# The written order of 3357 operations replaced by another in a convolution stem, forward and backward, on one core

## The chip, the cores and the metric

The kernel runs on one core of a Trainium2 chip. The metric is the device time of one launch in microseconds. Three runs of the kernel before took 1113.04, 1113.48 and 1116.73 us, median 1113.48. Five engines take part, each with its own queue of instructions that it works off in order: TensorE (PE, matmuls; its weight loads are listed as PEld), VectorE (DVE), ScalarE (ACT), GpSimd (POOL) and SyncE (SP), which here issues most of the DMAs.

## The reference

`x` is [2, 16000, 256], `w` is [31, 256, 256], `grad_out` is [2, 7985, 256], all bf16. A convolution with 31 taps and stride 2 is followed by a normalisation of each channel over the sequence and a tanh GELU; the outputs are its value and the gradients for x, w, gamma and beta.

```python
    L = (T - K) // s + 1
    h = jnp.einsum('blc,cd->bld', x[:, 0:s * L:s, :], w[0])
    for i in range(1, K):
        h = h + jnp.einsum('blc,cd->bld', x[:, i:i + s * L:s, :], w[i])
    mu = jnp.einsum('bld->bd', h)[:, None, :] / L
    var = jnp.einsum('bld->bd', (h - mu) ** 2)[:, None, :] / L
    h = (h - mu) / jnp.sqrt(var + 1e-5)
    h = h * gn_gamma[None, None, :] + gn_beta[None, None, :]
    return _gelu(h)
...
    _out, _vjp = jax.vjp(_f, x, w, gn_gamma, gn_beta)
    _grads = _vjp(grad_out)
    return (_out0, *[jnp.asarray(_g) for _g in _grads])
```

## The kernel before

The three convolutions (forward, gradient for x, gradient for w) are each cut by a fast FIR scheme: the 31 taps and the sequence are split into parts A and C and their sum B, twice nested, so that three products of half size stand for four. Products therefore need sums and differences of their operands first (VectorE) and of their results afterwards (VectorE, ScalarE).

The stages follow one another. F0 and F1 are the forward convolution of batch 0 and 1; the GELU and its derivative of batch 0 (`gelu_batch`) are worked off beside F1. Then follow G0 and G1, the gradient for x (`input_grad`), with the rest of the GELU of batch 1 beside it (`gelu_short`). W is last, the gradient for w (`weight_grad`), in nine combinations of parts; beside it, the late part of the output of batch 1 (`out0_late`) is made.

The code does not issue anything while it walks through these stages. `Plan.add` writes down each operation with its engine and a function that issues it, and finds out from the cells of SBUF and PSUM that it reads and writes which earlier operations it must follow. Then `Plan.order` reads a table, `SEQUENCE`, a list of the 3357 numbers, checks that each operation comes after those it must follow, and `emit` issues the operations in this order, held by `keep_in_program_order`. So the table alone sets the order of each engine's queue, the DMA issues on SyncE and GpSimd among them. Semaphores between engines are put in by the framework from the same dependences.

Names that the text below uses, with the lines that the profile gives:

- `load` (L314) issues a DMA, `turn` (L319) a transposing one; `x_first` (L408, L410) copies the first blocks of x, transposed by matmuls, out of PSUM.
- `w_sub` (L448) makes differences of weight parts, `f_sums` (L464) sums of x parts.
- `f_mm` (L506) issues the matmuls of the forward stage for one product: `f_leaf` the leaf products, `f_shared` those whose result two parts use. `f_copy` (L551) copies a result within PSUM on ScalarE, so that a second product can go on from it; `f_seed` (L581) does that with a VectorE pass. `f_evac` (L605, L611, L626) brings results out, with sums and squares for the statistics; `fwd_stats` (L804 to L816, root at L811) works these out.
- `keep` (L585) is ScalarE's copy of 1024 columns out of PSUM, wherever it is used.
- `w2_outer` (L1234, L1235) prepares weights for the gradient stage.
- `g_mm` (L1136) issues the matmuls of the gradient for x, `g_sums` (L1082) makes its operands. `g_copy` (L1165) is there what `f_copy` is in the forward stage: a matmul product, the copy on ScalarE, and then products that add to the copy. `g_seed` (L1199) is its VectorE form, `g_evac` (L1213, L1217) brings results out, and `load` stores them.
- `out0_late` (L964) applies GELU to a tile of batch 1 that was parked in DRAM (`hd`): load, activation on ScalarE, transposing DMA, store.
- `w_mm` (L1351) issues the matmuls of the gradient for w; `w_pairs` copies PSUM on ScalarE (L1453), `w_both` (L1461) seeds on VectorE; `leaf_d` (L1520, L1525), `pair_x` (L1417, L1421), `pair_d` (L1432, L1437) and `w_add` (L1316) make operands, and `w_emit` (L1380) brings results out. `arena` is the one SBUF buffer in which all tiles lie, `dld` and `vl` are DRAM buffers.

The loop that sets the order is

```python
        for i in self.order():
            r = self.ops[i]["fn"]()
            if hasattr(r, "__next__"):
                for ins in r:
                    pin(ins)
```

Of the kernel before, what the change touches and what calls it, by code (L numbers as in the profile page):

```python
# [39 lines left out]
7 10 4 1 11 8 5 9 2 13 3 6 12 20 14 15 36 30 38 39 29 35 32 40 33 31 24 34 37 23 41 42 50 48 47 45 21 51 44 49 46 43 22 53 59 54 26 52 64 28 60 83 84  # L40
25 65 82 18 86 85 27 66 16 62 19 67 91 17 70 55 87 79 88 58 63 92 76 251 94 56 61 57 68 89 69 180 77 95 179 71 90 177 96 73 97 98 72 242 99 178 107
100 101 194 193 102 267 108 189 93 103 127 263 116 109 190 111 141 110 78 112 104 117 113 142 114 115 143 121 198 122 105 144 74 118 119 157 124 145
123 195 75 158 126 181 153 125 183 167 197 154 146 155 159 166 156 81 160 169 162 120 163 185 147 128 182 184 164 106 80 196 165 168 176 148 175 149
150 223 161 152 222 151 187 171 204 191 170 225 129 363 199 224 203 234 213 206 130 192 273 200 361 205 271 201 255 362 214 207 132 188 209 274 377
216 133 215 131 226 366 260 275 202 210 373 211 367 212 208 287 186 218 360 227 217 219 276 220 172 134 221 324 283 277 288 325 284 285 286 233 378
293 364 292 290 228 289 295 135 279 278 232 294 231 379 280 302 281 136 296 291 282 297 326 298 137 340 299 365 138 327 301 300 380 330 328 350 139
331 368 349 374 140 336 329 381 370 333 337 338 341 339 173 351 303 264 345 376 505 332 346 344 334 372 352 343 270 353 382 507 347 174 358 348 342
383 257 229 359 369 250 230 304 386 384 387 0 305 335 385 405 306 354 506 406 417 388 307 504 407 390 389 396 392 308 418 309 371 397 355 393 258 394
520 521 400 408 375 399 402 395 431 409 310 419 247 391 415 410 411 401 420 356 404 508 414 403 398 427 416 311 422 428 357 423 312 468 429 432 313
412 421 430 425 434 510 433 441 469 511 413 235 440 314 315 443 484 316 424 523 470 442 426 436 512 444 435 437 317 471 239 516 524 438 472 439 485  # L50
446 445 475 517 474 318 509 494 319 480 473 320 321 525 476 481 486 477 478 493 482 487 483 490 479 322 489 488 323 492 522 514 491 518 496 638 503
526 495 447 532 502 497 637 531 498 530 550 519 499 636 551 552 527 533 562 528 635 553 448 529 534 500 449 537 535 563 450 536 515 576 451 564 538
539 648 541 540 554 513 546 555 639 545 547 556 542 452 640 549 453 544 559 565 548 641 543 572 566 561 577 573 454 245 593 652 568 579 642 501 567
560 643 570 574 592 578 569 575 557 594 582 656 586 558 644 581 455 571 602 585 456 583 580 584 645 587 597 237 588 457 654 591 595 589 590 598 596
611 599 621 459 607 458 460 655 600 608 601 603 612 615 605 609 610 650 620 613 646 614 616 461 606 657 617 623 622 625 618 604 633 624 619 634 462
681 682 626 683 463 663 629 658 464 662 651 653 918 665 704 659 627 672 684 628 660 664 691 668 666 466 630 631 661 467 920 649 669 676 647 670 686
465 671 678 667 924 685 677 921 687 922 680 632 679 934 690 923 688 705 673 919 730 693 941 931 674 675 930 942 689 933 692 967 932 694 926 695 696
697 698 948 935 699 925 236 940 936 700 701 702 968 703 927 707 937 708 938 709 928 943 950 929 710 969 706 711 944 714 712 957 949 966 945 713 715
946 716 947 939 954 717 953 731 726 956 733 718 955 952 719 958 965 722 720 723 725 724 721 729 973 959 734 1001 732 951 735 974 728 736 244 727 970
737 243 755 739 238 975 982 960 738 740 750 971 1007 976 252 741 991 751 972 961 986 756 742 743 978 999 992 979 744 980 758 962 745 746 754 747 981  # L60
748 988 1017 987 757 749 990 993 1024 989 759 753 241 1003 1002 780 977 752 983 1025 1004 1005 1006 760 1050 1013 985 761 984 1014 994 1000 1015 762
1016 995 1009 764 763 1008 998 765 1018 1023 776 1010 766 963 1011 767 1052 1019 783 768 1020 1012 1021 769 781 1027 772 771 770 1032 1026 773 775
774 782 779 784 1041 1028 785 1029 1022 786 1030 789 805 787 777 778 1037 1051 1036 788 790 1039 1031 1038 1034 791 1033 808 792 806 1049 1048 793
964 1042 794 799 796 795 1040 798 801 1057 1056 807 797 809 1043 830 810 1075 800 996 1053 997 811 804 1084 812 1054 1035 1065 1058 813 802 814 803
815 1055 831 816 1061 1059 817 1066 1062 1082 826 1044 1063 1077 818 1086 825 1064 1067 833 819 1071 1045 823 820 1070 824 1068 1073 821 1072 1069
832 1074 822 834 1083 857 827 1060 835 828 829 836 1101 1076 1091 1087 1085 1088 1089 1092 837 1090 1097 839 1096 838 1078 1099 840 1093 1046 1098
841 850 1094 1047 842 1103 268 1106 1081 1102 843 851 1095 1115 844 860 1100 846 854 1107 859 1116 1108 848 845 849 1136 861 1135 855 1114 1110 1118
847 858 862 1104 853 856 1111 863 1112 1125 884 866 864 852 1109 1134 1113 865 867 1120 1119 1079 868 1133 1122 1105 869 1121 1127 1124 1123 1117
1132 1131 870 885 871 1146 876 883 1126 877 873 874 875 1128 878 1145 886 1144 872 888 256 1141 887 889 1142 1170 1080 890 881 879 1148 1162 880 1143
1172 882 891 893 892 1153 1149 894 1154 895 1150 904 1151 1147 896 1163 905 1155 1156 897 1152 1157 898 1158 1165 1173 899 1159 1164 1137 1160 900  # L70
1161 1166 1174 1274 1171 906 907 901 1169 1175 1196 253 902 1195 1176 1198 1186 1182 1138 1197 903 1183 1184 1178 1185 1275 1202 1129 1289 1177 1203
1199 1180 1179 908 1291 909 1204 1292 1187 1276 1139 1191 910 1277 1189 1181 1192 1190 1205 1130 911 1200 1188 1193 1206 912 1140 1297 1167 1194 1298
1215 913 1201 1281 914 1219 1229 1216 1217 1208 1218 915 1278 1231 916 1294 1228 1293 1220 1207 1295 1230 1221 1168 1210 1296 1300 1321 1224 1299
1320 1212 1225 1290 1243 1213 1303 1226 1232 1301 1337 1227 1222 269 1302 1304 1209 1282 1244 1305 1306 1211 1523 1252 1214 1251 1223 1234 1254 1233
1235 1236 1358 1246 1285 1256 1237 1245 1239 1279 1238 1240 1241 1247 1524 1253 1323 1249 1248 1308 1255 1309 1250 1311 1242 1257 1312 1284 1260 1258
1313 1283 1261 1287 1310 1525 1259 1322 1526 1262 1280 1263 1531 1264 1527 1265 1532 1266 1324 1267 1315 1533 1325 1307 1327 1314 1268 1570 1537 1269
1318 1270 1271 1272 1316 1273 1317 1538 1571 1339 1539 1551 1319 1341 1326 1336 1543 1340 1528 1342 1529 1338 1288 1534 1530 1343 1544 1573 1572 1328
1286 1344 1578 1541 1345 1545 1329 1575 1542 1540 1346 1535 1330 1574 1548 1549 1331 1536 1579 1547 1347 1334 1550 1553 1648 1348 1649 1362 1349 1582
1559 1360 1350 1587 1580 1558 1352 1332 1583 1576 1552 1581 1356 1566 1586 1577 917 1546 1355 1554 1357 1560 1361 1565 1651 1555 1353 1363 1556 1650
1359 1606 1652 1561 1557 1364 1660 1607 1333 1564 1354 1585 1366 1563 1584 1562 1379 1589 1612 1365 1569 1335 1611 1629 1608 1653 1367 1630 1609 1654  # L80
1567 1655 1614 1590 1610 1368 1613 246 1616 1617 1595 1628 1369 1625 1618 1591 1370 1383 1623 1615 1371 1568 1598 1622 1657 1620 1656 1627 1594 1373
1381 1593 1619 1599 1631 1588 1377 1592 1624 1351 1658 1375 1378 1664 1376 1636 1384 1626 1380 1643 1601 1621 1382 1600 1665 1596 1632 1374 1385 1661
1637 1597 1633 1400 1668 1386 1712 1659 1674 1634 1387 1789 1644 1602 1635 1638 1388 1603 1641 1645 1666 1711 1389 1639 1667 1642 1790 1390 1640 1720
1404 1672 1647 1604 1673 1372 1391 1646 1669 1678 1719 1713 1670 1392 1605 1402 1675 1715 1394 1671 1676 1716 1679 1685 1398 1680 1399 1397 1684 1682
1681 1686 1403 1690 1792 1401 1405 1692 1795 1662 1714 1683 1406 1677 1724 1722 1691 1794 1408 1407 1663 1721 1393 1718 1688 1693 1717 1689 1409 1793
# [1608 lines left out]
```

## Time and profile before

| what | value |
|---|---|
| runs, median (lowest to highest) | 1113.48 us (1113.04 to 1116.73) |
| profiled execution, span | 1111.2 us |
| instructions in it | 18967 |
| VectorE busy | 919.9 us, 83% |
| ScalarE busy | 578.9 us, 52% |
| GpSimd busy | 129.3 us, 12% |
| DMA packets, volume | 348806, 256.16 MB |
| share of the 16 DMA engines, SyncE's hardware queue | 81.8% |
| granted TensorE clock | 1.00 in every stretch quoted below |

Of the profiled execution the page gives the span; the times of runs contain, beside the span, what lies around it. Busy times count an engine's instructions; TensorE's own row is quoted in the prediction. In rows of groups and of the timeline, brackets or the part behind the last bar tell how long the engine stood idle just before, and what it waited for. In a row of windows, each engine has its busy time and in parentheses its instructions.

### The profile page before, as it was taken

What the parts mean: (1) busy time and instruction counts of PE and PEld (TensorE: products, weight loads), DVE (VectorE), ACT (ScalarE), POOL (GpSimd) and SP (SyncE); (2) the same over time, 40 slices, a digit from 0 to 9 for tenths busy, and PEclk for the clock granted to TensorE, in tenths of its full rate; (3) what the DMA queues carried; (4) which work ended last, traced back from release to release, by engine and by line L of the source; (5) the groups of instructions that cost most, each with busy time, mean ns of one, the idle gap of its engine ahead of it and who ended that gap; (6) DMA issues with size and microseconds to landing.
All of it is one profiled execution on the core that took longest, in us unless ns stands there. A gap on an engine that the chain in (4) does not pass through costs nothing.

```text
span 1111.2 us, 18967 instructions
## 1 busy us (share of the span) xinstructions
PE 1086.2 (98%) x7623; PEld 749.8 (67%) x7672; DVE 919.9 (83%) x900; ACT 578.9 (52%) x880; POOL 129.3 (12%) x233
## 2 busy tenths in 40 slices
PE   6999999999999989999999999999999999999998
PEld 4888899878787974444444444444587776678885
DVE  7987877889999999989897565644789699699995
ACT  1234434587988569899964566545413322111221
POOL 0000000000001003232332432251200000000000
PEclk9999999999999999999999999999999999999999
DMA  9979899876969789999999898577994959978888
GB/s 231 198 188 249 233 275 267 219 167 162 209 166 219 240 328 270 274 252 265 217 225 237 179 203 183 157 201 197 278 293 137 270 156 298 303 254 279 282 253 207
DMA packets 348806, 256.16 MB, mean 231 GB/s; under 512 B 234327, under 2 KB 315869, under 8 KB 343517
## 3 DMA queue, kind: packets, MB, share of 16 engines
q1 hardware_dynamic: 341613, 236.05, 81.8%
q0 software_dynamic: 7104, 18.89, 6.3%
q8 instruction: 60, 0.98, 0.4%
q14 instruction: 29, 0.24, 0.1%
HBM read 114.62 MB, written 84.45 MB: 179 GB/s over the span
## 4 chain that ended last, share of the span: by engine, by line
PE 89%; DVE 5%; issue 2%; DMA 1%; SPq 1%; ACT 1%; DVEq 0%
PE ps L1136 34%; PE ps L506 34%; PE ps L1351 21%; SPq L314 1%; DMA out_dram<-arena 1%; DVE arena L1437 1%; DVE ps L1461 1%; DMA arena<-in_w_dram 1%; DVE arena L1421 1%; DVE arena L1380 1%; DVE arena L1525 0%; DVE arena L581 0%; DVE arena L1417 0%; DVE arena L448 0%; DVE arena L1316 0%
## 5 line engine op out<-in xcount | busy, mean ns | idle before, releaser
L506 PE MATMUL ps<-arena 128*128 128x256 bf16 (+4 forms) x3464 | 396.6, 278 | 11.2 <-DMA arena<-in_x_dram 4.7
L1136 PE MATMUL ps<-arena 128*128 128x512 bf16 (+1 forms) x1787 | 388.1, 376 | 5.7 <-ACT ps L1165 3.6
L506 PEld LDWEIGHTS <-arena 128*128 128x128 bf16 x3464 | 338.2, 98 | 69.4 <-DMA arena<-in_x_dram 5.8
L1136 PEld LDWEIGHTS <-arena 128*128 128x128 bf16 x1824 | 178.5, 98 | 215.1 <-issue 2.9
L1351 PE MATMUL ps<-arena 128*128 128x256 bf16 (+1 forms) x2372 | 301.6, 289 | 3.4 <-DVE arena L1520 1.8
L1351 PEld LDWEIGHTS <-arena 128*128 128x128 bf16 x2384 | 233.2, 98 | 71.9 <-issue 2.3
L585 ACT ACTIVATE arena<-ps 128x1024 bf16<-128x1024 f32 (+1 forms) x121 | 122.1, 1022 | 213.0 <-PE ps L1351 77.3
L464 DVE TENSOR_TENSOR arena<-arena 128x2064 bf16<-128x2064 bf16 (+7 forms) x131 | 162.7, 1265 | 24.2 <-PE ps L506 23.0
L314 POOL DMA_DIRECT2D dld<-arena x144 | 104.6, 728 | 246.7 <-DMA arena<-arena 229.4
L1199 DVE TENSOR_TENSOR ps<-ps,arena 128x1024 f32<-128x1024 f32 x36 | 44.3, 1232 | 64.2 <-PE ps L1136 53.2
L1082 DVE TENSOR_TENSOR arena<-arena 128x1032 bf16<-128x1032 bf16 (+1 forms) x114 | 89.5, 813 | 9.5 <-POOL arena L1049 4.3
L551 ACT ACTIVATE ps<-ps 128x256 f32<-128x256 f32 x89 | 36.7, 412 | 85.6 <-PE ps L506 84.5
L1316 DVE TENSOR_TENSOR arena<-arena 128x4096 bf16<-128x4096 bf16 x30 | 68.3, 2287 | 0.5 <-DMA arena<-in_x_dram 0.3
L1165 ACT COPY ps<-ps 128x512 f32<-128x512 f32 x84 | 48.1, 575 | 33.7 <-PE ps L1136 30.0
L323 POOL MEMSET arena<- 128x104 bf16 (+11 forms) x52 | 12.0, 249 | 414.8 <-DVE arena L464 157.6
L923 DVE TENSOR_TENSOR arena<-arena 128x2048 bf16<-128x2048 bf16 (+1 forms) x48 | 57.5, 1197 | 3.0 <-ACT arena L926 1.3
L605 ACT ACTIVATE arena<-ps 128x512 bf16<-128x512 f32 (+1 forms) x64 | 37.0, 582 | 32.7 <-PE ps L506 28.2
L885 DVE TENSOR_TENSOR arena<-arena 128x2048 bf16<-128x2048 bf16 (+1 forms) x40 | 47.7, 1197 | 4.0 <-ACT arena L879 1.7
L1437 DVE TENSOR_TENSOR arena<-arena 128x2048 bf16<-128x2048 bf16 x40 | 48.5, 1220 | 2.4 <-PE ps L1351 2.4
L1461 DVE TENSOR_TENSOR ps<-ps,arena 128x1024 f32<-128x1024 f32 x24 | 29.1, 1227 | 19.5 <-PE ps L1351 19.5
L1453 ACT COPY ps<-ps 128x256 f32<-128x256 f32 x54 | 19.0, 360 | 47.8 <-PE ps L1351 46.7
L1525 DVE TENSOR_TENSOR arena<-arena 128x4608 bf16<-128x4608 bf16 x16 | 40.6, 2554 | 0.0
(92 smaller groups left out, 752.3 us busy)
## 6 DMA issues: line engine op xcount, KB each, us to landing
arena<-in_x_dram SPq DMA_DIRECT2D x36, 1024.0 KB
arena<-hd SPq DMA_DIRECT2D x40, 512.0 KB
dld<-arena POOLq DMA_DIRECT2D x144, 128.0 KB, 4.4
out_dram<-arena SPq DMA_DIRECT2D x14, 1024.0 KB
arena<-dld SPq DMA_DIRECT2D x18, 640.0 KB
arena<-dld SPq DMA_DIRECT2D x18, 576.0 KB
vl<-arena SPq DMA_DIRECT2D x36, 256.0 KB
arena<-vl SPq DMA_DIRECT2D x9, 1024.0 KB
```

What stands on the lines that cost most here:

```text
L314: lambda: e.dma_start(out=out, in_=in_), dma=np_ * ns / 16e3 * 1.03, ns=ns, tp=SH[pk], slack=slack)
L464: lambda: nc.vector.tensor_tensor(out=o, in0=a, in1=b, op=ALU.add))
L506: yield nc.tensor.matmul(ps[:, dh, cs], lhsT=wt, rhs=mv, start=s0, stop=False, skip_group_check=True)
L585: lambda: nc.scalar.activation(out=out, in_=ps, func=ACT.Copy, scale=scale))
L885: add("DVE", dve(nf), [o], [a, b_], lambda: V.tensor_tensor(out=o, in0=a, in1=b_, op=op))
L923: add("DVE", dve(nf), [o], [a, b_], lambda: V.tensor_tensor(out=o, in0=a, in1=b_, op=op))
L1082: lambda: nc.vector.tensor_tensor(out=o, in0=a, in1=b, op=ALU.subtract))
L1136: yield nc.tensor.matmul(ps[:, e, 0:wide], lhsT=lt, rhs=mv, start=s0, stop=False, skip_group_check=True)
L1165: add("ACT", act(512), [o], [i], lambda: nc.scalar.copy(out=o, in_=i))
L1316: add("DVE", dve(4096), [o], [a, b], lambda: nc.vector.tensor_tensor(out=o, in0=a, in1=b, op=ALU.add))
L1351: yield nc.tensor.matmul(ps[:, s, c0:c1], lhsT=lt, rhs=mv, start=s0, stop=False, skip_group_check=True)
L1437: add("DVE", dve(2048), [o], [u, v], lambda o=o, u=u, v=v: nc.vector.tensor_tensor(out=o, in0=u, in1=v, op=ALU.subtract))
```

## The change

All 105 lines of the table are replaced by another permutation of the same 3357 numbers. Operations, dependences, buffers and all other code are the same. The first line of the table, before and after, stands for all:

```diff
 SEQUENCE = """
-7 10 4 1 11 8 5 9 2 13 3 6 12 20 14 15 36 30 38 39 29 35 32 40 33 31 24 34 37 23 41 42 50 48 47 45 21 51 44 49 46 43 22 53 59 54 26 52 64 28 60 83 84
+12 1 2 10 5 4 8 11 20 13 6 7 3 9 14 15 30 33 29 39 32 31 35 38 36 40 37 23 34 48 47 44 45 21 49 42 51 46 41 50 43 52 53 28 59 54 24 65 22 64 60 84 26
...
```

What moves is shown at three places. A row is one instruction or several alike (x and their number), with its line, operation, output and input.

SyncE, the start of the program: loads of x, of w and the first transposing loads. Before:

```order
L314 DMA arena<-in_x_dram 128x4x512 x2
L314 DMA arena<-in_x_dram 16x4x512
L314 DMA arena<-in_w_dram 128x4x256 x4
L314 DMA arena<-in_w_dram 128x3x256
L314 DMA arena<-in_w_dram 128x4x256 x4
```

and now:

```order
L314 DMA arena<-in_w_dram 128x4x256
L314 DMA arena<-in_x_dram 128x4x512 x2
L314 DMA arena<-in_w_dram 128x4x256
L314 DMA arena<-in_x_dram 16x4x512
L314 DMA arena<-in_w_dram 128x4x256 x4
```

One load of w has moved ahead of the two large first loads of x, and another ahead of the small one.

ScalarE, from the end of the forward convolution into the gradient for x. Before:

```order
L605 ACTIVATE arena,hsum_109<-ps 128x2x230 x3
L626 ACTIVATE arena,hsq_111<-arena 128x1024
L1165 COPY ps<-ps 128x512
L626 ACTIVATE arena,hsq_111<-arena 128x1024 x2
L1165 COPY ps<-ps 128x512
L1235 ACTIVATE arena<-arena 128x2048
L811 ACT_TABLE_LOAD
L811 ACTIVATE small<-small,eps_t 128x2
L1165 COPY ps<-ps 128x512
L585 ACTIVATE ps<-ps 128x1024
L1165 COPY arena<-ps 128x512
L916 ACTIVATE arena<-arena,stats 128x1024 x4
```

and now:

```order
L605 ACTIVATE arena,hsum_109<-ps 128x2x230 x2
L1165 COPY ps<-ps 128x512 x2
L626 ACTIVATE arena,hsq_111<-arena 128x1024 x2
L1165 COPY arena<-ps 128x512
L1165 COPY ps<-ps 128x512
L811 ACT_TABLE_LOAD
L811 ACTIVATE small<-small,eps_t 128x2
L585 ACTIVATE ps<-ps 128x1024
L916 ACTIVATE arena<-arena,stats 128x1024 x4
```

The two first copies now stand together ahead of the two squares, the copy to `arena` and the third copy stand ahead of the table load, and the pass of L1235 has moved out of the piece to an earlier place. On TensorE, whose rows all read alike here, the products were, by what they feed: first copy's producer, its consumer, second copy's producer, its two consumers, the third copy's producer, its two consumers. Now they are: first producer, second producer, a product of the outer part, a consumer of the second copy, the consumer of the first (the third copy's producer), the other consumer of the second, the two consumers of the third. At 485 us, too, a product has moved between the producer and the consumer of a copy, and at 199 us the four products that feed a seed (L581) have moved ahead of five others.

ScalarE, from the gradient for x (L585, L1165) into the gradient for w (L1453). Before:

```order
L1165 COPY ps<-ps 128x512 x2
L1165 COPY arena<-ps 128x512 x2
L585 ACTIVATE arena<-ps 128x2x512 x4
L1453 COPY ps<-ps 128x256 x6
L585 ACTIVATE arena<-ps 128x1024 x4
L1453 COPY ps<-ps 128x256
L585 ACTIVATE arena<-ps 128x1024
L1453 COPY ps<-ps 128x256 x5
L585 ACTIVATE arena<-ps 128x1024
L964 ACT_TABLE_LOAD
L964 ACTIVATE arena<-arena,stats 128x1024
```

and now:

```order
L1165 COPY arena<-ps 128x512
L585 ACTIVATE arena<-ps 128x2x512 x2
L964 ACT_TABLE_LOAD
L964 ACTIVATE arena<-arena,stats 128x1024
L585 ACTIVATE arena<-ps 128x2x512 x2
L1453 COPY ps<-ps 128x256 x6
L585 ACTIVATE arena<-ps 128x1024 x3
L964 ACTIVATE arena<-arena,stats 128x1024
```

The first activation of `out0_late` and the table load that it needs have moved from behind the copies of the second combination of W to between the last two pairs of evacuations of the gradient for x. Its load from `hd` has moved with it on SyncE, ahead of a load of the d tile.

208 rows, old and new, of the table SEQUENCE are left out of this document.

## The prediction

> **What bounds the kernel now.** I read the page first (span, busy times, chain), then the waits of TensorE, then the chain and the timeline around each long wait. Columns of the busy line: busy us, share of the span, instructions.
>
> ```profile
> span 1111.2 us, 18967 instructions
> PE 1086.2 (98%) x7623; PEld 749.8 (67%) x7672; DVE 919.9 (83%) x900; ACT 578.9 (52%) x880; POOL 129.3 (12%) x233
> PE 89%; DVE 5%; issue 2%; DMA 1%; SPq 1%; ACT 1%; DVEq 0%
> ```
>
> TensorE is busy 1086.2 of 1111.2 us and carries 89% of the chain that ended last. The change leaves all operations as they are, so those 1086 us stay. Only the rest can shrink: 1111.2 − 1086.2 = 25.0 us. Its named part is in the waits of TensorE (us in total, times, longest):
>
> ```profile
> PE ps L506 <- DMA arena<-in_x_dram: 4.7, 1, 4.7
> PE ps L1136 <- ACT ps L1165: 3.6, 4, 1.1
> PE ps L1351 <- DVE arena L1520: 1.8, 1, 1.8
> PE ps L506 <- DVE arena L448: 1.7, 2, 1.1
> PE ps L506 <- DVE ps L581: 1.4, 1, 1.4
> PE ps L506 <- DVE arena L464: 1.3, 1, 1.3
> PE ps L1351 <- DVE arena L1421: 1.0, 1, 1.0
> PE ps L506 <- DVE arena L410: 0.7, 1, 0.7
> PE ps L506 <- ACT arena L408: 0.7, 1, 0.7
> PE ps L506 <- ACT ps L551: 0.7, 1, 0.7
> ```
>
> These sum to 17.6 us. Of them 4.7 is the first load, before which nothing can be multiplied. The last stretch of matmuls in the timeline (start, length, what, count, idle before) is
>
> ```profile
> 1073.30 33.20 PE L1351 MATMUL ps<-arena 128*128 128x256 bf16 x238 [0.99 <-DVE arena L1421]
> ```
>
> and ends at 1106.5, so another 4.7 us is the tail. What a better order can win is therefore the other 12.9 us at most, 1.2% of the span. No wait but the first names a DMA directly. The wait for L1520 has one behind it, below. A plan that only gives transfers more room finds little to win here; what it moves for that can cost.
>
> **The change, place by place.** Base is the profiled execution, span 1111.2; the median of the runs, 1113.48, lies 2.3 us above it, which I take as the time around the span and the same for both kernels. So each term is added to 1113.5.
>
> *Start (0 to 37 us).* In SyncE's new order one load of w stands ahead of the two first loads of x. The first issues, two waits of TensorE, and the page's row of ScalarE's copies (busy, mean ns, idle before):
>
> ```profile
> 0.74 2.04 SPq L314 DMA_DIRECT2D arena<-in_x_dram  x3
> 16.28 9.18 PE L506 MATMUL ps<-arena 128*128 128x512 bf16 x60 [1.08 <-DVE arena L448]
> 26.06 10.67 PE L506 MATMUL ps<-arena 128*128 128x256 bf16 x88 [0.60 <-DVE arena L448]
> L551 ACT ACTIVATE ps<-ps 128x256 f32<-128x256 f32 x89 | 36.7, 412 | 85.6 <-PE ps L506 84.5
> ```
>
> Three issues in 2.04 are 0.68 us each, so the first x lands about 0.7 later, and 256 KB of w share the engines with it: +0.7. On TensorE two short leaf products (8 matmuls of 256 columns, 8 × 10.67 / 88 = 1.0 us each) now stand in the wait at 16.28. They need less than what they are put ahead of, but VectorE must still make its operands; of the 1.08 I leave 0.5. A leaf product of twice that length is moved up ahead of 26.06 and covers that wait, 0.6. But the leaf product that stood behind the shared product at 26.06, as cover for ScalarE's copies of it (L551, 412 ns), is now later, so the next products follow the shared one directly and wait for two copies and the handover: +1.0, bounded by the present 0.7 for L551 and three copies, 1.2. Sum 0.7 − 0.6 − 0.6 + 1.0 = **+0.5** (−0.6 to +1.5).
>
> *Second forward batch (199 us).*
>
> ```profile
> 197.77 1.23 DVE L581 TENSOR_TENSOR ps<-arena,ps 128x1024 f32<-128x1024 f32 x1 [0.52 <-PE ps L506]
> 199.06 2.15 PE L506 MATMUL ps<-arena 128*128 128x231 bf16 x20 [1.39 <-DVE ps L581]
> ```
>
> VectorE's seed starts after the last product on that PSUM and TensorE has nothing but its consumer. The new order does that group first and puts five other products between, of 8 matmuls like those of the row (8 × 2.15 / 20 = 0.86 us), 4.3 in all: the 1.39 goes. What is late next is another product seeded by a second 1.23 us pass, behind one product; I leave 0.3 for it. **−1.1** (−1.4 to −0.6).
>
> *From forward to input gradient (407 to 418 us).* Pieces of the chain that ended last here (start, length, what):
>
> ```profile
> 409.95 1.15 ACT arena L626 x2
> ...
> 412.27 0.48 ACT ps L1165
> 412.75 1.84 ACT arena L1235
> 414.59 0.02 issue
> 414.61 1.28 ACT L811
> ```
>
> ScalarE paces it: squares for the statistics (L626), one 1.84 us pass (L1235) and a table load (L811) stand ahead of copies (L1165) that TensorE waits for. Three waits of the 3.6 us row lie here, 2.9 in all (the fourth, 0.7, is at 485). The new order puts L1235 some 14 rows earlier on ScalarE, joins the two first copies ahead of two squares, and puts other products between a copy's producer and consumer on TensorE. What is left: on ScalarE the third copy to ps stands behind the first two, two squares and a copy to arena. From the last forward product on the second copy cannot end before two products and itself, 2 × 0.86 + 0.57 = 2.3; the squares add 2.2 and the next two copies 1.2, 5.7 us in all. TensorE has six products of four matmuls, 0.86 each (working below), before it needs the third copy, 5.2: 0.5 left. Then the table load, its root and a keep of 1.02 end some 2.6 after it, with two products, 1.7, as cover: 0.9 left if all of that comes in a row, 0 if the keep is early, taken 0.5. So 1.0 of 2.9 stays: **−1.9** (−2.9 to −0.3).
>
> *At 485 us.*
>
> ```profile
> 484.89 0.57 ACT L1165 COPY ps<-ps 128x512 f32<-128x512 f32 x1 [0.40 <-PE ps L1136]
> 485.51 2.75 PE L1136 MATMUL ps<-arena 128*128 128x512 bf16 x11 [0.66 <-ACT ps L1165]
> ```
>
> The consumer of the copy stood right behind its producer; now one product stands between: **−0.7** (−0.8 to 0).
>
> *The rest of the input gradient.* This is where the new order gives something back. Windows (us, busy and instructions of PE, PEld, DVE, ACT, POOL, clock, DMA share, GB/s):
>
> ```profile
> 417.00:475.00 58.00, 57.74 (x270) 26.70 (x274) 56.53 (x66) 52.24 (x59) 17.91 (x25) 1.00 1.07 272
> 490.00:797.00 307.00, 305.53 (x1411) 140.83 (x1439) 206.41 (x236) 196.57 (x254) 92.73 (x162) 1.00 0.87 211
> ```
>
> TensorE loses 1.5 us in 307 now. A four-matmul product is 4 × 57.74 / 270 = 0.86; a copy with its handovers cost TensorE 0.66 of waiting at 485.51. Before, most consumers of a copy have two products between them and their producer, about 1.7 us; in the new order some 45 have exactly one. One product just covers a copy when ScalarE is free, and does not when a keep (L585, 1.02 us in the rows below) has just begun. ScalarE is busy 196.57 of 307 us here, 64%. None of the 45 may collide (0), or one in ten for a whole keep (4.5). The order puts copies ahead of keeps at most of these places, so I take the end nearest to the present row, one collision: **+1.0** (0 to +4.5).
>
> *From input gradient to weight gradient (797 to 816 us).*
>
> ```profile
> 802.78 1.24 DVE arena L1213
> 804.02 0.02 issue
> 804.03 6.89 DMA out_dram<-arena
> ```
>
> then two passes of L1520 and the 1.75 us wait of TensorE at 813.92. Keep, evacuation, store, buffer free, d planes: this chain has no slack (the keep at 801.73 is quoted below). In the new order ScalarE gets a table load and the first late GELU (L964) between the two pairs of keeps at its head. Present prices and present gaps:
>
> ```profile
> L964 ACT ACTIVATE arena<-arena,stats x16: 1224/1240/1263, 842.2 to 1092.8; 128x1024 bf16<-128x1024 bf16 x16
> L964 ACT ACT_TABLE_LOAD  x1: 1283/1283/1283, 840.9 to 840.9; - x1
>   DMA arena<-hd: 31.2, 2
> 800.00 1.02 ACT L585 ACTIVATE arena<-ps 128x1024 bf16<-128x1024 f32 x1 [0.65 <-PE ps L1136]
> 801.73 1.02 ACT L585 ACTIVATE arena<-ps 128x1024 bf16<-128x1024 f32 x1 [0.70 <-PE ps L1136]
> ```
>
> 1.28 + 1.24 = 2.52, less the two gaps 0.65 + 0.70 = 1.35, leaves 1.2 by which the second keep, and with it the store and TensorE's wait, is late; 0.1 more for three copies behind it. At 840 the same pair delayed nobody. **+1.3** (0, if the store no longer ends last, to +5, rival two).
>
> The Trainium skill ("ScalarE: Activation LUTs", section "What ACT_TABLE_LOAD costs") gives 1283 ns for the load and about 1380 ns for a drain with it. By that, an estimate, this term would be +2.7 and the time 1114.0. This case's trace has the 1283 ns and no drain: the first GELU began at 842.2, 1.3 us after the load at 840.9.
>
> *VectorE's stretch and the tail.*
>
> ```profile
> 1000.00:1073.00 73.00, 72.30 (x634) 61.84 (x632) 72.66 (x54) 13.64 (x21) 0.00 (x0) 1.00 0.85 274
> ```
>
> VectorE is full (72.66 of 73) and the wait of 1.0 at 1073 is its. The same passes must come before the same product, so an order can neither help nor harm: 0 (−0.9 to +1). The tail, 4.7 us, is the last evacuation and stores and stays.
>
> Sum: 0.5 − 1.1 − 1.9 − 0.7 + 1.0 + 1.3 = −0.9, so 1113.5 − 0.9 = 1112.6.
>
> **The rivals.** *One: the waits go and nothing comes back.* For it: all of the waits removed are short round trips, and the new order does put products into each. Against it: the one-product distances and L964 in the chain. Without the two plus terms, and with all 2.9 at 407 to 418 gone: 0.5 − 1.1 − 2.9 − 0.7 = −4.2, 1109.3.
>
> *Two, slower: the load behind L964.*
>
> ```profile
> 797.00:816.00 19.00, 17.20 (x137) 13.30 (x137) 15.75 (x14) 8.07 (x12) 2.88 (x4) 1.00 1.03 229
> ```
>
> ScalarE takes its queue in order. The GELU needs a 512 KB load from hd, issued shortly before 797. If it has not landed when the keep ahead of it ends (799.4), ScalarE stands, and the next keeps, the evacuation, the store and TensorE's wait are late by the same time. ScalarE waited 31.2 us in two such waits before, without harm since nothing hung on it; by this window's row the DMA engines move 229 GB/s at a share of 1.03 in this stretch, so 512 KB take 2.3 us. One such length late, and the store's 6.89 longer by another: 1.3 + 2.3 + 2.3 = 5.9 in place of 1.3, so 1112.6 + 4.6 = 1117.2; with three or four collisions in the input gradient too, 1120. It decides from a lateness of 2.1 us that the store shares: 2 × 2.1 takes 1112.6 over 1116.8. Against it: the new order puts the load on SyncE ahead of the last loads of the d tile for the next stage, so it has several us before 799.4.
>
> *Three: the order misses its plan.* Loads and stores on SyncE's queue are moved by up to hundreds of us; one that now lands late makes a wait that the trace of before cannot show. Each would cost 1 to 3 us, and collisions of copies and keeps add to them: 1114 to 1119. If the waits also stay where they are because real times differ from the plan's, the time is 1113.5.
>
> **How the numbers follow.** Chances: forecast (1110.2 to 1116) 0.40; rival one (1106 to 1110.1) 0.30; rival two (1117 to 1121) 0.15; rival three 0.15, half of it within 0.3% and half above. A measurement of this kernel tells about 0.3% from no change, 3.3 us, so faster is below 1110.1 and slower above 1116.8: faster 0.30, same 0.40 + 0.08 = 0.48, slower 0.15 + 0.07 = 0.22. The range 1107 to 1119 leaves out the best third of rival one and the upper half of rival two, less than 2 in 10.
>
> **What would show it.** The waits of TensorE: L581 no longer at 1.4; L1165 from 3.6 to below 2 around 408 to 418, but with new short entries between 490 and 797; L1520 grown from 1.8 to about 3; L551 with a second entry near 28 us; the first load later than 4.68. VectorE's and ScalarE's busy times must be unchanged. If L1520's wait is gone or not longer, the term for L964 is wrong; if ScalarE stands more than 2 us for hd near 800, rival two holds; if a DMA is named among TensorE's waits after the first, rival three. Wrong altogether would be a time below 1106, since it would need the matmul work itself or the tail to shrink.

## The result and the profile after

| | before | changed |
|---|---|---|
| runs, median (lowest to highest) | 1114.14 us (1113.04 to 1116.73) | 1132.56 us (1128.09 to 1134.99) |
| profiled execution, span | 1111.2 us | 1133.2 us |
| ratio to before, 95% interval | | 1.0157 (1.0132 to 1.0183) |

The new order is 1.6% slower, 18 us, where no change was forecast and the range ended at 1119. (The kernel before has four runs here; its median over three, 1113.48, is what the prediction starts from.) First the page of the changed kernel, then the waits of TensorE (us in total, times, longest):

```profile
span 1133.2 us, 18998 instructions
PE 1092.2 (96%) x7622; PEld 749.9 (66%) x7672; DVE 925.3 (82%) x900; ACT 581.8 (51%) x880; POOL 127.7 (11%) x233
```

```profile
PE ps L1136 <- DVE ps L1199: 7.6, 5, 5.6
PE ps L506 <- DMA arena<-in_x_dram: 6.3, 1, 6.3
PE ps L1136 <- ACT ps L1165: 2.7, 4, 1.4
PE ps L1136 <- ACT arena L585: 2.5, 2, 1.4
PE ps L506 <- DVE arena L464: 2.5, 3, 1.9
PE ps L1136 <- DVE arena L1217: 2.4, 2, 1.4
PE ps L506 <- ACT ps L551: 2.2, 3, 0.9
PE ps L1351 <- DVE arena L1520: 1.4, 1, 1.4
PE ps L1136 <- DVE stats L987: 1.0, 1, 1.0
...
PE ps L506 <- DVE ps L581: 0.8, 1, 0.8
```

What was 3.6 us for L1136 is now a whole family: the seed L1199, the copy L1165, the keep L585, the evacuation L1217, and more. Still no DMA but the first load is named. The window of the gradient for x, from its first product to the first of the gradient for w, shows where the time lies (columns as in the prediction; before, then changed):

```profile
408.02:801.52 393.50, 387.96 (x1787) 178.59 (x1825) 290.39 (x339) 274.80 (x345) 118.22 (x201) 1.00 0.91 225
```

```profile
410.39:823.99 413.60, 393.30 (x1789) 178.62 (x1824) 293.35 (x340) 275.48 (x348) 117.90 (x203) 0.99 0.88 219
```

413.6 against 393.5: 20.1 us of the 22.0 by which the spans differ. TensorE is idle for 20.3 of them in place of 5.5, and its busy time is 5.3 longer for the same products, some of which ran at a lower granted clock (last section). Ahead of this stage the new order is 2.4 late, behind it 0.5 early.

So one asks what VectorE and ScalarE waited for in this stretch. Before, their waits name no DMA at all; two rows name GpSimd (4.3 and 1.6 us). In the changed kernel, VectorE's and ScalarE's waits between 410 and 824 us:

```profile
DVE arena L1316 <- DMA arena<-in_x_dram: 9.2, 1, 9.2
DVE arena L1017 <- DMA arena<-dyd: 6.6, 4, 2.0
DVE arena L1015 <- DMA arena<-hd: 3.4, 2, 2.3
DVE arena L1217 <- DMA out_dram<-arena: 3.0, 1, 3.0
DVE arena L1082 <- DMA arena<-arena: 2.1, 1, 2.1
DVE arena L1234 <- DMA dld<-arena: 1.4, 1, 1.4
ACT arena L916 <- DMA arena<-hd: 4.6, 2, 3.8
ACT arena L1024 <- DMA arena<-dyd: 3.2, 2, 2.5
ACT L964 <- DMA arena<-hd: 2.2, 1, 2.2
```

These sum to 35.7 us. GpSimd is named for 12.9 us, where it was 5.9. Here is one of the waits for a load, in SyncE's and ScalarE's timeline of the changed kernel:

```profile
666.59 0.58 SPq L314 DMA_DIRECT2D arena<-dyd  x1
```

```profile
670.33 1.15 ACT L1024 ACTIVATE arena<-arena,stats 128x1024 bf16<-128x1024 bf16 x1 [2.51 <-DMA arena<-dyd]
671.38 1.92 ACT L585 ACTIVATE arena<-ps 128x1024 bf16<-128x1024 f32 x2
```

The load is issued at 666.59, its first user could run 1.2 us later, when ScalarE was free, and starts 3.7 later. Two keeps stand behind it on ScalarE, and TensorE waits 1.1 us for the first. Before, the same load went out 7.1 us ahead of the first operation that needs it, and ScalarE did not wait:

```profile
645.21 0.32 SPq L314 DMA_DIRECT2D arena<-dyd  x1
```

```profile
652.29 1.16 ACT L1024 ACTIVATE arena<-arena,stats 128x1024 bf16<-128x1024 bf16 x1
```

The longest wait, in the chain that ended last and on TensorE's timeline of the changed kernel:

```profile
803.35 11.47 DMA arena<-in_x_dram
...
814.91 0.06 DVE arena L1316
814.97 2.15 issue
817.12 1.23 DVE ps L1199
```

```profile
818.40 5.76 PE L1136 MATMUL ps<-arena 128*128 128x512 bf16 x16 [5.63 <-DVE ps L1199]
```

A sum for the gradient for w (L1316) waits for a load of x that takes 11.5 us beside two others of 1 MB, and the last seed of the gradient for x (L1199) stands behind it on VectorE. VectorE was free for the sum at 805.69, 2.3 us after the load went out at 803.35. Before, the same load had 9.0 us, and the sum did not wait:

```profile
787.28 0.58 SPq L314 DMA_DIRECT2D arena<-in_x_dram  x1
```

```profile
796.24 2.28 DVE L1316 TENSOR_TENSOR arena<-arena 128x4096 bf16<-128x4096 bf16 x1
```

### The profile page after: what moved, and what is told of

It reads as the page before. It is cut to its first block, busy times and chain, and to the rows that moved or that the text cites. A ratio compares the mean times of both kernels' runs of the same rounds, so it can differ in the third digit from the quotient of the medians.

```text
span 1133.2 us, 18998 instructions
## 1 busy us (share of the span) xinstructions
PE 1092.2 (96%) x7622; PEld 749.9 (66%) x7672; DVE 925.3 (82%) x900; ACT 581.8 (51%) x880; POOL 127.7 (11%) x233
## 5 line engine op out<-in xcount | busy, mean ns | idle before, releaser
L1136 PE MATMUL ps<-arena 128*128 128x512 bf16 (+1 forms) x1787 | 393.5, 378 | 20.3 <-DVE ps L1199 7.6
L1136 PEld LDWEIGHTS <-arena 128*128 128x128 bf16 x1824 | 178.6, 98 | 234.8 <-issue 25.2
L585 ACT ACTIVATE arena<-ps 128x1024 bf16<-128x1024 f32 (+1 forms) x121 | 121.3, 1021 | 221.3 <-PE ps L1351 90.9
L464 DVE TENSOR_TENSOR arena<-arena 128x2064 bf16<-128x2064 bf16 (+8 forms) x131 | 163.1, 1263 | 10.7 <-PE ps L506 6.3
L1082 DVE TENSOR_TENSOR arena<-arena 128x1032 bf16<-128x1032 bf16 (+1 forms) x114 | 89.5, 813 | 19.1 <-PE ps L1136 8.7
L1316 DVE TENSOR_TENSOR arena<-arena 128x4096 bf16<-128x4096 bf16 x30 | 68.2, 2284 | 20.4 <-DMA arena<-in_x_dram 20.1
L1199 DVE TENSOR_TENSOR ps<-ps,arena 128x1024 f32<-128x1024 f32 x36 | 44.2, 1229 | 39.2 <-PE ps L1136 27.6
L1165 ACT COPY ps<-ps 128x512 f32<-128x512 f32 x84 | 48.0, 573 | 38.7 <-PE ps L1136 35.7
L551 ACT ACTIVATE ps<-ps 128x256 f32<-128x256 f32 (+1 forms) x89 | 36.3, 410 | 59.8 <-PE ps L506 58.3
L323 POOL MEMSET arena<- 128x78 bf16 (+11 forms) x52 | 11.4, 244 | 377.7 <-DVE arena L885 151.2
L1437 DVE TENSOR_TENSOR arena<-arena 128x2048 bf16<-128x2048 bf16 x40 | 48.2, 1217 | 5.2 <-PE ps L1351 4.8
L964 ACT ACTIVATE arena<-arena,stats 128x1024 bf16<-128x1024 bf16 x16 | 19.3, 1236 | 54.2 <-DMA arena<-hd 54.2
L1213 DVE TENSOR_TENSOR arena<-arena 128x2048 bf16<-128x2048 bf16 x20 | 24.4, 1221 | 24.3 <-ACT arena L585 24.3
```

Source lines behind the costliest of these rows:

```text
L464: lambda: nc.vector.tensor_tensor(out=o, in0=a, in1=b, op=ALU.add))
L585: lambda: nc.scalar.activation(out=out, in_=ps, func=ACT.Copy, scale=scale))
L1082: lambda: nc.vector.tensor_tensor(out=o, in0=a, in1=b, op=ALU.subtract))
L1136: yield nc.tensor.matmul(ps[:, e, 0:wide], lhsT=lt, rhs=mv, start=s0, stop=False, skip_group_check=True)
L1165: add("ACT", act(512), [o], [i], lambda: nc.scalar.copy(out=o, in_=i))
L1316: add("DVE", dve(4096), [o], [a, b], lambda: nc.vector.tensor_tensor(out=o, in0=a, in1=b, op=ALU.add))
```

## The experiments

**Which stage.** Four splices of the two orders: up to a cut one order, from there the other. The first has its cut at operation 1311, the first product of the gradient for x; a piece of the table around it, old order, then spliced:

```diff
-1248 1308 1255 1309 1250 1311 1242 1257 1312 1284
+1280 1283 1527 1242 1284 1311 1287 1533 1525 1257
```

*e1*, old, then new.

> The order of before up to the first product of the gradient for x (407 us), the new order from there to the end. Theory one (the loss lies in the gradient for x: from its first to its last product the new order took 413.5 us, the old 393.3) expects about +20 us over the kernel before, within 4. Rival (the loss starts in the forward stage, where the new order was already 2.3 us late, and is carried on) expects +10 or less.

Measured: 1131.57 us against 1113.81, ratio 1.016 (1.0137 to 1.0183): +18. *e3*, the other way round at the same cut:

> The new order up to the first product of the gradient for x, the old order from there. Theory one expects +0 to +3 us against the kernel before: 2.3 late at that place, of which the old order behind it gives nothing back. Rival (the leftover of the forward stage sets the gradient's waits) expects +10 us or more.

Measured: 1114.94, ratio 1.0007 (0.9997 to 1.0018). So at most some 2 us of the 18 begin in the forward stage. *e16* goes over to the old order only at 1970, in the middle of the gradient for x:

```diff
-1915 1982 1511 1512 1988 1970 2027 1983 1939 2026
+1981 1913 1915 1982 1988 1970 2027 1983 1939 2026
```

> The new order to the end of the gradient for x of batch 0 (575 us), the old order from there. By the stages of the traces (new against old: forward +2.3, batch 0 +4.7, batch 1 +15.5, gradient for w -0.5) theory two expects +5 to +8 us. Rival (the loss of batch 1 comes from leftovers of batch 0) expects +15 us or more.

Measured: 1123.6 against 1114.09, ratio 1.0094 (1.0079 to 1.0109), +9.5, somewhat more than the 5 to 8 that were expected and far from the rival's 15. About half of the loss stands by the end of batch 0, so both batches lose. *e2* takes the old order up to the first product of the gradient for w, 2771:

```diff
-2751 2750 2752 2782 2780 2771 2753 2783 2776 2754
+2705 2707 2872 2875 2704 2771 2753 2781 2708 2776
```

> The order of before up to the first product of the gradient for w (801 us), the new order from there. Theory one (nothing lost in the gradient for w, 309.4 against 309.9 us) expects -1 to +1 us against the kernel before. Rival (the new order's loads for this stage come too late whatever stood ahead) expects +3 us or more.

Measured: 1125.71, ratio 1.011 (1.0095 to 1.0125): +12, where -1 to +1 was expected. The cut made it: the load from hd (2872) that the new order issues ahead of this stage now goes out behind the cut, with its GELU (2875) close behind. One of TensorE's waits in e2, and what ScalarE did:

```profile
PE ps L1351 <- ACT ps L1453: 10.8, 1, 10.8
```

```profile
813.06 1.28 ACT L964 ACT_TABLE_LOAD   x1 [10.46 <-DMA arena<-hd]
```

The copies of L1453 stood behind L964, which waited for its load. This is the prediction's second rival, as an artefact of the splice. It says nothing on the new order's last stage, which in the trace of the changed kernel takes 0.5 us less than before.

**Heads of queues.** The first theory was that operations which wait for a transfer merely stand ahead of what TensorE needs. *e4* swaps two operations on VectorE:

```diff
-L1199 TENSOR_TENSOR ps<-ps,arena 128x1024
-L1316 TENSOR_TENSOR arena<-arena 128x4096
-L1199 TENSOR_TENSOR ps<-ps,arena 128x1024
+L1199 TENSOR_TENSOR ps<-ps,arena 128x1024 x2
+L1316 TENSOR_TENSOR arena<-arena 128x4096
```

> The new order with one operation moved by one place on VectorE: the sum of x blocks for the gradient for w (L1316), which waited 9.2 us for its load with the last seed but one of the gradient for x (L1199) behind it, goes behind that seed. Theory one (one sum at the head of the queue costs the 5.6 us wait of TensorE at 818 and the 2.3 us by which the next 16 matmuls ran slower) expects 7 to 9 us less than the changed kernel, so about +10 us over the kernel before, and a granted clock of 1.00. Rival (the load is late anyway, and the wait moves to the first product of the gradient for w that needs the sum) expects 2 us less or nothing.

Measured: 1133.17 (1127.96 to 1139.77), nothing gained. The 5.6 us wait is gone from the trace, but the next one has grown, from 1.4 us:

```profile
PE ps L1351 <- DVE arena L1520: 4.1, 1, 4.1
```

*e5* mends six such places further up; two of the six as rows:

```diff
-L1017 TENSOR_SCALAR arena<-arena,stats 128x2048
 L1217 TENSOR_TENSOR arena<-ps,arena 128x2x512
+L1017 TENSOR_SCALAR arena<-arena,stats 128x2048
...
-L1024 ACTIVATE arena<-arena,stats 128x1024
 L585 ACTIVATE arena<-ps 128x2x512 x2
+L1024 ACTIVATE arena<-arena,stats 128x1024
```

> The new order with six places of the gradient for x mended, the boundary to the gradient for w left alone. At each, an operation that waits for a transfer steps behind the evacuation, seed or copy that stood behind it: on VectorE L1017 twice (waited 2.0 and 1.7 us for a load), L1015 to L1033 once (1.1), on ScalarE L1024 (2.5), on GpSimd two stores behind three fills (VectorE waited 1.6 for them); and on SyncE a store to out_dram goes ahead of three transposing loads (VectorE waited 3.0 for it). Theory one (each of these waits was handed on to TensorE whole or in part: 1.05, 1.03, 0.95, 1.12, 1.41 and 1.39 us there) expects 5 to 8 us less than the changed kernel, about 1126. Rival (VectorE and ScalarE are simply too full in this stretch, and another wait of the same size takes each place) expects 2 us less or nothing.

Measured: 1132.1. *e6*, e4 and the late GELU:

```diff
-L964 ACT_TABLE_LOAD
-L964 ACTIVATE arena<-arena,stats 128x1024
 L585 ACTIVATE arena<-ps 128x2x512 x2
 L1453 COPY ps<-ps 128x256 x6
+L964 ACT_TABLE_LOAD
+L964 ACTIVATE arena<-arena,stats 128x1024
```

> The new order with the sum of L1316 behind the seed, as in e4_swap_back, and the first late GELU (L964), with its table load, behind the six copies of L1453 instead of ahead of two keeps. Theory one (queue heads that wait for a load: what e4 took away at 818 us partly came back as a longer wait at 828, since the keeps stand behind L964, whose load from hd lands late in some runs) expects 1124 to 1127 us and a spread of runs below 5 us, where e4 had 1128 to 1140. Rival (the store of the last evacuation and the loads of x land late by themselves) expects the 1128 to 1140 of e4 again.

Measured: 1135.02 (1128.4 to 1135.72). *e7*, e5 and e6 together:

> The new order with the edits of e5 and e6 together. Theory one expects the sum of both, 1132 - 6 - 7, about 1118 to 1121 us; the rest over the kernel before is then the later start (1.6) and waits that were not mended (L1235 at 587, 1.4 to 2.5). Rival (too much work at these places) expects no more than the better of the two.

Measured: 1135.6 (1130.87 to 1139.88). Theory one fell three times over. In e6's trace the waits at the mended places are gone or short, and TensorE waits at the first products of the gradient for w instead, for L1520 and for loads of that stage by name:

```profile
PE ps L1351 <- DVE arena L1520: 5.8, 1, 5.8
PE ps L1351 <- DMA arena<-dld: 3.4, 2, 2.0
```

**Transfers.** Theory two: the transfers themselves are late. *e9* sorts the queues of SyncE and GpSimd between 410 and 830 us by readiness; 180 of SyncE's operations and 165 of GpSimd's move, by 10 places at most. The first piece:

```diff
-L314 DMA arena<-vl_57 128x4096
+L314 DMA arena<-hd_0_64 128x2x1024
+L314 DMA arena<-vl_57 128x4096 x2
 L314 DMA hd_3_67<-arena 128x4096
-L314 DMA arena<-hd_0_64 128x2x1024
```

> The new order with only the queues of SyncE and GpSimd sorted anew between 410 and 830 us: each load, transposing load and store goes out in the order in which its inputs or its buffer were ready in the trace of the changed kernel (at most 12 us ahead of where it stood); the queues of TensorE, VectorE and ScalarE stay. Theory two (mending heads of queues did nothing because the transfers themselves are issued too late: VectorE and ScalarE waited 0 us for DMAs in the gradient for x before, and 36 us now; leads of 6.6 to 15.7 us before are 0.9 to 5.8 now, while a load needs 5 to 8) expects 5 to 10 us less than the changed kernel, for those transfers that stood ready behind others. Rival (they are late because the new order of VectorE and ScalarE sets their buffers free too late, so no order on SyncE helps) expects within 2 us of the changed kernel.

Measured: 1133.25, ratio 1.0175 (1.0158 to 1.0193). But the lateness is still there: the waits of VectorE and ScalarE for DMAs in this stretch sum to 32 us, where the changed kernel had 36. *e10*, e9 and e7 together:

> The edits of e9 and of e7 together: transfers in order of readiness, and what waits for one behind what TensorE waits for. Theory two expects less than e9, about 1117 to 1122 us, since now both the lateness and its handing on are cut. Rival (buffers too late) expects the 1131 to 1140 us of e7.

Measured: 1133.01. Sorting SyncE's and GpSimd's queues gives nothing back either, as the rivals of e9 and e10 had it. *e12* goes the other way and makes the old order late; two of its twelve moves, both on SyncE, are *e15*. The second of these two is:

```diff
-L319 DMA_TRANSPOSE arena<-arena 128x4x128 x8
-L314 DMA arena<-dyd_2_74 128x2048
-L319 DMA_TRANSPOSE arena<-arena 128x4x128
+L319 DMA_TRANSPOSE arena<-arena 128x4x128 x9
 L314 DMA out_dram<-arena 104x4096
 L319 DMA_TRANSPOSE arena<-arena 128x4x128 x2
 L314 DMA arena<-hd_2_66 128x2048
 L314 DMA dld_7_83<-zt_114 2x256
-L319 DMA_TRANSPOSE arena<-arena 128x4x128 x5
+L319 DMA_TRANSPOSE arena<-arena 128x4x128 x4
+L314 DMA arena<-dyd_2_74 128x2048
+L319 DMA_TRANSPOSE arena<-arena 128x4x128
```

> The order of before with eleven transfers of the gradient for x on SyncE and one on GpSimd moved back in their queue by 0 to 10 places, by the time that their lead over their user is shorter in the new order (2.6 to 14.7 us); all compute queues stay. Theory two expects waits of VectorE and ScalarE for these transfers as in the changed kernel, some 10 to 20 us in all, and 4 to 10 us more than the kernel before. Rival (the new order of the compute queues is what costs) expects 0 to 1 us more.

Measured: 1129.54 against 1114.13, ratio 1.0131 (1.0099 to 1.0163): +15, more than the 4 to 10 expected. The waits of VectorE and ScalarE for DMAs sum to 17 us, as expected.

> The order of before with two of the twelve transfers of e12 moved back alone: a load of hd for the GELU (by 3 places on SyncE) and a load of dyd (by 10). In e12 TensorE waited 4.2 and 5.5 us behind these two, and ran at a granted clock of 0.75 and 0.54 for the 5.5 us after each. Theory (a wait of 4 us or more is paid about one and a half times) expects 9.7 of waits and 3 to 4 of slow clock, +11 to +14 us over the kernel before. Rival (the loss of e12 comes from all twelve together) expects +3 us or less.

Measured: 1122.78 against 1114.09, ratio 1.0087 (1.0066 to 1.0107): +8.7 for two loads out of 3357 operations, less than the 11 to 14 expected and far more than the rival's 3. The waits were shorter than in e12: in e15 TensorE waited 3.9 and 3.0 us for the keeps behind the two loads' users:

```profile
PE ps L1136 <- ACT arena L585: 3.9, 1, 3.9
PE ps L1136 <- ACT ps L585: 3.0, 1, 3.0
```

**The loads taken away.** *e13* is the new order without 42 loads, *e14* the old one without them (line numbers of both are 3 higher from `emit` on):

```diff
+        leave = set([1291, 1292, 1298, 1320,
...
         for i in self.order():
+            if i in leave:
+                continue
```

> The new order without 42 loads that VectorE and ScalarE wait for in the gradient for x: those of dyd and hd for its operands and its GELU, and the last two of x and the first of hd for the gradient for w. What they would fetch is left out, and the operations go on with what the tiles hold. Theory two (late loads are the cause) expects most of the 20 us back: within 2 to 6 us of e14. Rival (the order of the compute queues is the cause) expects 12 to 18 us more than e14.

> The order of before without the same 42 loads, as a control for e13. Both theories expect no change against the kernel before, within 1 us, since VectorE and ScalarE waited for no DMA in this stretch.

Measured, against 1114.09: e13 1116.15, ratio 1.0017 (1.0007 to 1.0027); e14 1114.53, ratio 0.9999 (0.9988 to 1.0011). The control does not move, and 16 of the 18 us are gone. GpSimd, too, is named for 3.3 us in place of 12.9. TensorE's timeline of e13, up to the gradient for w:

```profile
411.47 2.83 PE L1139 MATMUL ps<-arena 128*128 128x512 bf16 x11
...
433.52 370.87 PE L1139 MATMUL ps<-arena 128*128 128x512 bf16 x1697 [0.17 <-DVE arena L923]
804.23 10.64 PE L1354 MATMUL ps<-arena 128*128 128x256 bf16 x96
```

From 433.5 to 804.2 not one wait of TensorE is listed. The stage takes 392.8 us, where the old order takes 393.5. So the new order of VectorE, ScalarE and TensorE is as good as the old one there, the one-product distances included, once the loads are out of it. That the loads cost by coming late, and not only by their volume, is what e12 and e15 show: all their loads are there, and only places in a queue differ.

**Moves to keep?** *e8* took two of the new order's moves on TensorE, the first of them in part, into the old order (numbers of operations in TensorE's queue):

```diff
-612 620 616 617 623 622 618 619 681
+612 620 616 617 618 619 623 622 681
...
-1689 1695 1702
+1695 1689 1702
```

> The order of before with two of the new order's moves on TensorE alone: at 199 us the four products that feed the seed (L581) go ahead of two others, and at 485 us one product goes between a copy (L1165) and its producer. Theory (these two waits, 1.39 and 0.66 us, go and nothing comes back) expects 1.5 to 2 us less than the kernel before. Rival (the wait at 199 only moves, as the new order showed 0.8 us at another seed, at 219) expects 0 to 1 us less.

Measured: 1116.97 against 1113.95, ratio 1.0025 (1.0015 to 1.0035), 3 us more. The wait at 199 us grew by 1.0, since VectorE's queue kept a sum (L464) that needs operation 622 ahead of the seed, and the granted clock behind it was 0.72 for 5.5 us, 1.5 us more (last section). At 485 us a wait of 0.5 for an evacuation (L1217) took the place of the 0.66 for the copy. Both in TensorE's waits in e8:

```profile
PE ps L506 <- DVE ps L581: 2.4, 1, 2.4
...
PE ps L1136 <- DVE arena L1217: 0.5, 1, 0.5
```

*e11* moves the seed too, and leaves out the move at 485:

```diff
-L464 TENSOR_TENSOR arena<-arena 128x8x232
-L581 TENSOR_TENSOR ps<-arena,ps 128x1024
+L581 TENSOR_TENSOR ps<-arena,ps 128x1024
+L464 TENSOR_TENSOR arena<-arena 128x8x232
```

> The order of before with the move at 199 us done on both queues: the four products that feed the seed (L581) go ahead of two others on TensorE, and on VectorE the seed goes ahead of the sum (L464) that waits for one of those two. In e8 only TensorE's part was moved, and its wait there grew from 1.39 to 2.35 us behind that sum. Theory (the wait at 199 is a plain round trip) expects 1 to 1.4 us less than the kernel before. Rival expects no change.

Measured: 1113.03 against 1114.13, ratio 0.9992 (0.9983 to 1.0001). The row for L581 is gone from TensorE's waits; the row for L464 grew from 1.3 to 1.9. This is the best version found, but its interval reaches no change.

## Why the prediction was wrong

- *What bounds the kernel*: the products stay, but "those 1086 us stay" was wrong: TensorE is busy 1092.2 us in the new order, in part because of the lower granted clock behind the longest wait. Whether 12.9 us can be won no run shows; the best version (e11) has a median 1.1 lower, with an interval that reaches no change. I wrote that "No wait but the first names a DMA directly" and drew from it that transfers had room to spare. They had some, and that room was the thing at stake: a reserve does not show as a wait until it is gone.
- *Start*, +0.5: the terms were off and the sum close. The first load came 1.6 us later (6.3 against 4.7), not 0.7; both waits for L448 went, where half of one was to stay; L551 got its second wait, 0.92 at 30.22, as forecast. At the wait that both orders share, 37.41 became 38.05: +0.6.
- *199 us*, −1.1: the wait of 1.39 went. A seed elsewhere took 0.8 (L581), a miss of the kind "what is late next" in another place than I looked. All told the forward stage came out 2.4 later, not 0.6 earlier; e3 puts it at 1.1, with an interval that reaches no change.
- *407 to 418 us*, −1.9: right. Of 2.9 for L1165 there, 0.8 is left, 0.25 named for L1082 and 0.57 for the keep L585; I had said 1.0. *485 us*, −0.7: that wait went.
- *The rest of the input gradient*, +1.0, at most +4.5: **this is the step that failed.** I counted distances between copies and products and let ScalarE's keeps collide with copies. e13 shows that the one-product distances cost nothing. What I did not count is the distance between each load and its first user, in queue places on SyncE against queue places on VectorE and ScalarE; the sum has no term for it, and only rival three speaks of it. For the load of dyd above, 7.1 us became 1.2, for the load of x 9.0 became 2.3. The stage from the first product of the gradient for x to the first of the gradient for w lost 20 us, and TensorE's waits for what stood behind such loads, with the clock they cost, are what e13 took away.
- *From input gradient to weight gradient*, +1.3: the wait for L1520 shrank (1.75 to 1.38) instead of growing to 3, so by the prediction's own sign the term was wrong. A larger wait, 5.6 us, came 18 us earlier, at a seed behind L1316. L964 with its table load was not what bound there: ScalarE waited 2.2 for its load, inside TensorE's longer wait for the seed. (More than 2 us was the sign for rival two; the wait came, but it is not what TensorE waited for.) The Trainium skill ("ScalarE: Activation LUTs", section "What ACT_TABLE_LOAD costs") puts a drain of about 1380 ns beside the table load. None showed here either: the load takes 1.28 us and the GELU follows it at once, in ScalarE's timeline:

```profile
816.33 1.28 ACT L964 ACT_TABLE_LOAD   x1 [2.23 <-DMA arena<-hd]
817.62 1.24 ACT L964 ACTIVATE arena<-arena,stats 128x1024 bf16<-128x1024 bf16 x1
```

- *VectorE's stretch and the tail*, 0: right; from the first product of the gradient for w to the end the new order takes 0.5 us less, of which L1520 has 0.4. The busy times of VectorE and ScalarE, forecast as unchanged, rose by 5.4 and 2.9 us; no run looks into that.
- *The rivals*: the second had the mechanism, a load at the head of an in-order queue with TensorE's work behind it, at one place and at 1117. The third, "the order misses its plan", had the cause, with 0.15 and at most 1119: I priced a few late loads, there were a dozen, and I took a wait's price for its length. Its sign for the reader, a DMA among TensorE's own waits, was wrong too: the DMAs are named one step back, in the waits of VectorE and ScalarE.

What stays open is why each load is late in the new order. Some stood ready behind others: the load of dyd at 666.59 had its buffer free 10 us earlier by the trace, with transposing loads ahead of it. Others went out as soon as their buffer was free, because the operation that frees it had moved toward the next user. e9 set out to mend the first kind alone; it brought the waits for DMAs down only from 36 to 32 us and gained nothing. The second kind was not undone by itself. e13 also spares the DMA engines the volume of 42 loads. How much of its gain that is was not measured apart; the control e14 shows only that the old order has no use for it.

## What to carry to other kernels

Before an order of instructions is changed, list for each load its lead, from issue to the end of what stands ahead of its user, and hold it against how long such loads take in the trace; a kernel that waits for no DMA has leads worth keeping. A late load behind an in-order queue must be mended at the load: moving its user back only hands the wait on. And an order is one thing over all queues: the move at 199 us made on TensorE alone (e8) lengthened the wait there from 1.4 to 2.4 us, and made on two queues (e11) it took that wait away.

## What the runs showed of the hardware

A long wait of TensorE can be paid a second time, by a lower granted clock behind it. Here are windows behind waits of 2.4 us (e8), 2.7 us (e12), 3.0 and 3.9 us (e15) and 5.6 us (the changed kernel), in this order; the clock is the third number from the end:

```profile
200.50:206.00 5.50, 5.50 (x41) 4.80 (x41) 5.50 (x6) 0.00 (x0) 0.00 (x0) 0.72 0.35 126
```

```profile
831.50:837.00 5.50, 5.49 (x51) 4.92 (x51) 5.50 (x5) 0.00 (x0) 0.00 (x0) 1.00 0.96 333
```

```profile
505.10:510.60 5.50, 5.48 (x27) 2.63 (x27) 4.81 (x6) 5.47 (x5) 0.81 (x2) 1.00 1.04 297
665.00:670.50 5.50, 5.27 (x18) 2.19 (x19) 2.52 (x3) 3.02 (x4) 2.41 (x4) 0.74 0.73 192
```

```profile
818.40:824.10 5.70, 5.70 (x18) 2.17 (x17) 4.10 (x5) 1.49 (x2) 4.45 (x7) 0.62 1.05 402
```

After 2.4 us the clock was 0.72, after 2.7 and after 3.0 us 1.00, after 3.9 us 0.74 and after 5.6 us 0.62. Over these windows of 5.5 and 5.7 us the three lower values cost 1.5, 1.4 and 2.2 us more. The Trainium skill ("TensorE: Matmul & The Clock Gate", section "Part 1: The HAM clock gate") puts the fall at one idle window of about 3.4 us. The waits of e12, of e15 and of the changed kernel lie on the sides that it gives; that of e8 does not, and neither does a wait of 2.1 us in e14, behind which the clock was 0.69 for 5.5 us:

```profile
814.70:820.20 5.50, 5.50 (x36) 4.29 (x36) 5.50 (x5) 0.00 (x0) 0.00 (x0) 0.69 1.03 370
```

So a wait of TensorE between 2 and 3 us was already paid twice in some of these runs, and its length alone did not say in which.
